# One decode step on one core: semaphores cleared beside the output's flight, and another order of loads in the last head

## The chip, the cores and the metric

One core of a Trainium2 chip. The metric is the device time of one execution in microseconds (us). The span that the profile shows runs from the first to the last instruction of the program; it is 1.7 to 2.9 us shorter than the time. The profile shows the granted clock of TensorE as a share of full speed: at every instant of the profile of before it is 1.0 or 0.5 (mean over the span 0.884).

## The reference

A token passes a layer norm, 32 heads of attention over 32,768 cached keys and values of 192 elements each, and an MLP of 640 to 1,536 to 640, with residuals.

```python
q = (layernorm(x) @ wq).reshape(B, Sq, H, Dh)         # 32 heads of 192
scores = einsum("bhqd,bhkd->bhqk", q, k_cache) * Dh ** -0.5
o = einsum("bhqk,bhkd->bhqd", softmax(scores), v_cache)
h = x + o.reshape(...) @ wo
out = h + relu(layernorm(h) @ w1) @ w2
```

The keys and values are 805 MB of the 825 MB that must be read.

## The kernel before

SyncE issues the loads (all but the token's own 1.25 KB) from one list. GpSimd passes on their arrivals. Per head, TensorE transposes a part of the keys and scores them, ScalarE copies the transposed keys out of PSUM and takes exponentials, VectorE scores the rest of the keys by multiplying and reducing, and TensorE sums the values. The last head is cut into ten chunks, numbered 0 to 9, so that little is left to do when the stream ends. Its order of loads:

```python
        end_keys(2, 2 * P * JL, JL, "dk1")
        g.wait("PV", LAST - 1, NC - 1)                 # values of the head before are used
        end_values(1, 0, JL * Dh, "dva", "v", LAST, 1) # "second values": chunks 2 and 3
        for i, jl in enumerate(ENDJ):                  # "last keys": chunks 6 to 9
            end_keys(NL - 1 + i, k0, jl, f"dke{1 + i}")
        ...                                            # more values, then w1 and w2
        g.wait("y_row")
        load(out.rearrange("b s (c p) -> (b s c) p", p=P), y_row[:], "dout", "out")
        g.wait("out")                                  # SyncE waits for the output here
        g.do(lambda: nc.sync.nop())
```

TensorE in the last head (the argument after `h` is the chunk):

```python
        transposes(g, h, 5)
        scores_pe(g, h, 4)
        values(g, h, 2)
        scores_pe(g, h, 5)
        transposes(g, h, 6)
        values(g, h, 3)
        ...
        values(g, h, 4)
        scores_pe(g, h, 8)
        scores_pe(g, h, 9)
        for c in (5, 6, 7):
            values(g, h, c)
        den_mm(g, h)                                   # the softmax's denominator
        values(g, h, 8)
        values(g, h, 9)
```

ScalarE there copies a chunk's transposed keys (`copies`), then takes the exponential of TensorE's scores (`exp_pe`) and of VectorE's (`exp_dve`) of a chunk or two earlier, in one fixed order. At the end of the program the context `nc.cleanup_on_exit()` lets GpSimd clear the 40 semaphores and then makes all engines meet once more (at a meeting each engine waits until all have come); before it there is the meeting that ends the block, after it the exit of the critical section and the program's last meeting.

The softmax here doesn't subtract the row's maximum and nothing guards it: scores larger than these inputs give would overflow.

Of the kernel before, what the change touches and what calls it, by code (L numbers as in the profile page):

```python
# [80 lines left out]
def kernel(  # L81
# [12 lines left out]
    nc = tc.nc  # L94
# [3 lines left out]
    _, H, Sk, Dh = A_k_cache.shape  # L98
# [9 lines left out]
    JL = 64  # L108
# [5 lines left out]
    NC = 2 * NL  # L114
    NB = NC
    LAST = H - 1
# [11 lines left out]
    NCM = len(ends)  # L128

    def chunks(h):  # L130
        return ends if h == LAST else full
# [14 lines left out]
    wo_view = A_wo.rearrange("(g p b) n -> g p b n", p=P, b=3)  # L146

    ctx.enter_context(tc.tile_critical(name="decode", no_gpsimd_drain=True))
    ctx.enter_context(nc.cleanup_on_exit())

    def sbuf(name, shape, dtype, align=32):
        return ctx.enter_context(nc.sbuf_tensor(name, shape, dtype, align_bytes=align))
# [77 lines left out]
    def dma_program(g):  # L230
        def load(dst, src, sem, *label):
            g.do(lambda: nc.sync.dma_start(out=dst, in_=src), sem, label, by=16)

        def rows(src, h, k0, jl):
            return src[h, k0:k0 + P * jl, :].rearrange("(p j) d -> p (j d)", p=P)

        def keys(h, ld):
            if h > 0:
                if ld == 0:
                    g.wait("PV", h - 1, 4 if h == 1 else 2)  # L240
                else:
                    g.wait("PV", h - 1, 5)
                g.wait("scs", h - 1, 4 * ld + 3)
            elif ld == 1:
                g.wait("att0")
            load(kt[ld][:], rows(k_hd, h, P * JK * ld, JK), f"dk{ld}", "k", h, ld)

        def vals(h, ld):

            if ld == 1:  # L250
                g.wait("PV", h, 1)
            elif h > 0:
                g.wait("PV", h - 1, 3 if ld == 0 else NC - 1)
            src = rows(v_hd, h, P * JK * (ld // 2), JK)
            if ld < 2:
                src = src[:, ld * JL * Dh:(ld + 1) * JL * Dh]
            load((vb, vb, va)[ld][:], src, "dva" if ld == 2 else "dvb", "v", h, ld)

        for c in range(DT):
            load(wq_c[c], wq_view[:, c * H * Dh:(c + 1) * H * Dh], f"dwq{c}", "wq", c)  # L260
        for h in range(LAST):
            keys(h, 0)
            vals(h, 0)
            keys(h, 1)
            for ld in ((2, 1) if h == 0 else (1, 2)):
                vals(h, ld)
            if h % 2 == 0:
                if h > 0:
                    g.wait("prj", h)
                load(wo_s[:], wo_view[h // 2], "dwo", "wo", h // 2)  # L270

        def end_keys(i, k0, jl, sem):
            load(k_at[i], rows(k_hd, LAST, k0, jl), sem, "k", LAST, i)

        def end_values(ld, c0, c1, sem, *label):
            load(v_at[ld][:, c0:c1], rows(v_hd, LAST, P * JL * ld, JL)[:, c0:c1], sem, *label)


        g.wait("PV", LAST - 1, 2)
        g.wait("scs", LAST - 1, 3)  # L280
        end_keys(0, 0, JL, "dk0")
        g.wait("PV", LAST - 1, 3)
        end_values(0, 0, JL * Dh, "dvb", "v", LAST, 0)
        end_keys(1, P * JL, JL, "dke0")
        g.wait("PV", LAST - 1, 5)
        g.wait("scs", LAST - 1, NC - 1)
        end_keys(2, 2 * P * JL, JL, "dk1")
        g.wait("PV", LAST - 1, NC - 1)
        end_values(1, 0, JL * Dh, "dva", "v", LAST, 1)
        k0 = P * JL * (NL - 1)  # L290
        at = []
        for i, jl in enumerate(ENDJ):
            at.append((k0, jl))
            end_keys(NL - 1 + i, k0, jl, f"dke{1 + i}")
            k0 += P * jl

        for i in range(2):
            end_values(2, i * J * Dh, (i + 1) * J * Dh, f"dvh{i}", "vh", i)
        i = 0
        for ld, (k0, jl) in enumerate(at):  # L300
            for c, (l, off, jc, *_) in enumerate(ends):
                if l == NL - 1 + ld:
                    g.wait("PV", LAST, 1)
                    load(v_tile(LAST, l)[:, off * Dh:(off + jc) * Dh],
                         rows(v_hd, LAST, k0, jl)[:, off * Dh:(off + jc) * Dh], f"dve{i}", "vc", LAST, c)
                    i += 1
        g.wait("PV", LAST, 3)
        load(w1_s, B_w1.rearrange("(c p) n -> p c n", p=P), "dw1", "w1")
        for i, (c0, c1) in enumerate(zip(W2_CUTS[:-1], W2_CUTS[1:])):
            load(w2_s[:, c0:c1], B_w2.rearrange("(c p) n -> p c n", p=P)[:, c0:c1], f"dw2_{i}", "w2", i)  # L310
        g.wait("y_row")
        load(out.rearrange("b s (c p) -> (b s c) p", p=P), y_row[:], "dout", "out")
        g.wait("out")
        g.do(lambda: nc.sync.nop())


    def pool_program(g):
# [225 lines left out]
    def pe_end(g):  # L543
        h = LAST
        den_mm(g, h - 1)
        transposes(g, h, 0)
        transposes(g, h, 1)
        scores_pe(g, h, 0)
        values(g, h, 0)
        scores_pe(g, h, 1)  # L550
        transposes(g, h, 2)
        o_turn(g, h - 1)
        values(g, h, 1)
        scores_pe(g, h, 2)
        transposes(g, h, 3)
        transposes(g, h, 4)
        scores_pe(g, h, 3)
        transposes(g, h, 5)
        scores_pe(g, h, 4)
        values(g, h, 2)  # L560
        scores_pe(g, h, 5)
        transposes(g, h, 6)
        values(g, h, 3)
        transposes(g, h, 7)
        scores_pe(g, h, 6)
        transposes(g, h, 8)
        scores_pe(g, h, 7)
        transposes(g, h, 9)
        values(g, h, 4)
        scores_pe(g, h, 8)  # L570
        scores_pe(g, h, 9)
        for c in (5, 6, 7):
            values(g, h, c)
        den_mm(g, h)
        values(g, h, 8)
        values(g, h, 9)
        o_turn(g, h)
        project(g, h + 1)
        st = ln_t["ln2"]["st"]
        g.wait("h_col")  # L580
        pe_group(g, [mmul(mm[:, 0:1], mean_mat[:], st[:, 0:1], start=True, stop=True)], ("mean", "ln2"), "pe_dve")
        g.wait("st", "ln2")
        pe_group(g, [mmul(sp[:, 0:2], mean_mat[:], st[:], start=True, stop=True)], ("mean2",), "pe_dve")
        g.wait("xn", "ln2")
        g.wait("w1")
        hn = ln_t["ln2"]["xn"]
        pe_group(g, [mmul(o_ps[:, f:f + 1], w1_s[:, c, f * P:(f + 1) * P], hn[:, c:c + 1],
                          start=(c == 0), stop=(c == DT - 1)) for f in range(FT) for c in range(DT)], ("h1",), "pe_act")
        g.wait("h1T")
        for i, (f0, f1) in enumerate(zip(W2_CUTS[:-1], W2_CUTS[1:])):  # L590
            g.wait("w2", i)
            pe_group(g, [mmul(attT[:, n:n + 1], w2_s[:, f, n * P:(n + 1) * P], h1T[:, f:f + 1],
                              start=(f == 0 and n == 0), stop=(f == FT - 1 and n == DT - 1), skip_group_check=True)
                         for f in range(f0, f1) for n in range(DT)], ("y", i), "pe_dve")
        g.wait("y_col")
        pe_group(g, [lambda: pe.transpose(out=mm[0:DT, 0:P], in_=y_col[:], identity=ident_f[:])], ("yT",), "pe_dve")
# [28 lines left out]
    def q_wide(g, h):  # L625
        g.wait("qs", h)
        if h > 0:
            g.wait("sc", h - 1, NC - 1)
        g.do(lambda: act.copy(out=qb[:], in_=mm[:, 0:Dh]), "act_dve", ("qb", h))
        g.do(lambda: act.copy(out=qm[:], in_=mm[:, Dh:Dh + 12]), "act_pe", ("qm", h))  # L630
# [12 lines left out]

    def act_head(g, h):
        q_wide(g, h)

        n = len(chunks(h))
        for c in range(n):
            if c == 4 and h < LAST:
                exp_pe(g, h, 3)  # L650
                exp_dve(g, h, 3)
                copies(g, h, 4)
                continue
            copies(g, h, c)
            if h == LAST:
                if c > 2:
                    exp_pe(g, h, c - 1)
                if c > 5:
                    exp_dve(g, h, c - 2)
                if c < 2:  # L660
                    exp_pe(g, h, c)
                    exp_dve(g, h, c)
                elif 2 < c < 5:
                    exp_dve(g, h, c - 1)
            elif c > 0:
                exp_pe(g, h, c - 1)
                exp_dve(g, h, c - 1)
        exp_pe(g, h, n - 1)
        if h == LAST:
            exp_dve(g, h, n - 2)  # L670
        exp_dve(g, h, n - 1)

    def act_end(g):
        act_head(g, LAST)
# [202 lines left out]
            looped("pe", nc.tensor)  # L877


# [1 line left out]
_INS = ['A_x', 'A_k_cache', 'A_v_cache', 'A_wq', 'A_wo', 'B_x', 'B_w1', 'B_w2']  # L881
_OUTS = [((1, 1, 640), 'bfloat16')]
# [25 lines left out]
```

## Time and profile before

| | before |
|---|---|
| time, median of 3 | 1918.56 us (1918.42 to 1918.67) |
| span of the profiled execution | 1916.9 us |
| loads' queue | 99.8% of the span |
| VectorE, TensorE, ScalarE busy | 82%, 81%, 49% |
| last head's first keys landed | 1849.97 us |
| denominator's matmul starts | 1903.35 us |
| output issued | 1913.29 us |
| last instruction ends | 1916.92 us |

A kernel with a full load queue is read from its end. The four last rows are the marks that profiles are compared by. The first comes from the semaphore records of the landings, the others from the order in time.

### The profile page before, as it was taken

To read this page: it belongs to the slowest core of one execution; us is meant where nothing else is said; L and a number is where in the kernel's file an instruction comes from. 1 tells how busy PE (TensorE), PEld (TensorE's weight loads), DVE (VectorE), ACT (ScalarE), POOL (GpSimd) and SP (SyncE) were. 2 spreads that over 40 slices of the span, in tenths; PEclk is the share of its full clock that TensorE was granted. 3 is DMA by queue.
4 is the path that set the end of the run, shared out by engine and by line. 5 is a ranking of instruction groups with operands and counts; after the bars stand their busy time and mean duration, and the time that the engine had idled before them with its cause. 6 is when DMAs were issued, how large, how long until landed. Compare 5 with 4: busy or idle time off the path is not lost.

```text
span 1916.9 us, 36096 instructions
## 1 busy us (share of the span) xinstructions
PE 1549.2 (81%) x15890; PEld 1083.9 (57%) x15890; DVE 1563.2 (82%) x732; ACT 938.9 (49%) x1998; POOL 1.0 (0%) x6
## 2 busy tenths in 40 slices
PE   7778787887878788878878877878778787878887
PEld 7555555655555555555556555556555555555555
DVE  2797787987878978789787888878798787887897
ACT  2455454554544544545545445445455454454454
POOL 0000000000000000000000000000000000000000
PEclk9888998888988889888899888899888898888988
DMA  9999999999999999999999999999999999999998
GB/s 408 429 432 434 429 437 428 439 432 432 434 435 431 434 436 428 436 431 438 433 434 435 432 433 434 435 428 438 429 437 434 432 436 432 433 435 433 430 430 354
DMA packets 29634, 825.29 MB, mean 431 GB/s; under 512 B 3115, under 2 KB 4652, under 8 KB 8108
## 3 DMA queue, kind: packets, MB, share of 16 engines
q1 hardware_dynamic: 29610, 824.98, 99.8%
q8 instruction: 15, 0.25, 0.0%
q14 instruction: 7, 0.06, 0.0%
q10 hardware_dynamic: 2, 0.00, 0.0%
HBM read 824.97 MB, written 0.00 MB: 430 GB/s over the span
## 4 chain that ended last, share of the span: by engine, by line
DVE 42%; DMA 37%; PE 14%; ACT 5%; issue 1%; DVEq 0%; POOLq 0%; SPq 0%
DMA kt<-in_A_k_cache_dram 35%; DVE sc L704 20%; DVE pr L701 20%; PE o_ps L364 7%; PE tp L383 6%; ACT kT L607 5%; DMA va<-in_A_v_cache_dram 2%; DVE o_pair L716 1%; PE sp L364 1%; ACT pA L622 0%; DVE oT L726 0%; DMA kt<-in_A_wq_dram 0%; DVE rec L709 0%; DVE rec L710 0%; DVE odd L722 0%
## 5 line engine op out<-in xcount | busy, mean ns | idle before, releaser
L701 DVE TENSOR_TENSOR pr<-kt,qb 128x3072 f32<-128x3072 bf16 (+2 forms) x257 | 757.5, 2947 | 314.8 <-POOLq L325 286.7
L607 ACT COPY kT<-tp 128x1024 bf16<-128x1024 bf16 (+1 forms) x897 | 813.2, 1016 | 277.3 <-PE tp L383 277.2
L383 PE MATMUL tp<-ident_f,kt 128*128 128x128 f32 x3453 | 586.2, 330 | 239.5 <-POOLq L346 164.2
L704 DVE TENSOR_REDUCE sc<-pr 128x16 f32<-128x3072 f32 (+2 forms) x257 | 756.9, 2945 | 8.9
L383 PEld LDWEIGHTS tp<-ident_f,kt 128*128 128x128 f32 x3453 | 481.2, 170 | 290.8 <-POOLq L346 169.7
L364 PE MATMUL o_ps<-va,pB 128*2 128x384 bf16 x1150 | 221.3, 340 | 66.2 <-POOLq L346 66.2
L364 PEld LDWEIGHTS sp<-qm,kT 128*128 128x128 bf16 x6906 | 197.4, 98 | 84.0 <-issue 43.0
L364 PE MATMUL sp<-qm,kT 128*128 128x2 bf16 x6906 | 214.4, 164 | 26.6 <-ACT pB L613 25.2
L364 PE MATMUL o_ps<-vb,pB 128*2 128x384 bf16 x1152 | 213.6, 331 | 23.1 <-ACT pA L622 22.5
L622 ACT ACTIVATE pA<-sc 128x16 bf16<-128x16 f32 (+2 forms) x257 | 58.1, 226 | 350.3 <-DVEq L65 350.2
L613 ACT ACTIVATE pB<-sp 128x16 bf16<-128x16 f32 (+2 forms) x258 | 51.9, 201 | 303.8 <-PE sp L364 303.8
L364 PEld LDWEIGHTS o_ps<-va,pB 128*2 128x2 bf16 x1150 | 93.9, 86 | 161.8 <-POOLq L346 73.7
L364 PE MATMUL o_ps<-va,pA 128*2 128x384 bf16 x898 | 173.5, 335 | 0.0
L364 PE MATMUL o_ps<-vb,pA 128*2 128x384 bf16 x896 | 166.7, 326 | 0.0
L364 PEld LDWEIGHTS o_ps<-vb,pB 128*2 128x2 bf16 x1152 | 90.0, 84 | 122.3 <-ACT pA L622 28.4
L364 PEld LDWEIGHTS o_ps<-va,pA 128*2 128x2 bf16 x898 | 77.7, 87 | 77.1 <-issue 11.3
L364 PEld LDWEIGHTS o_ps<-vb,pA 128*2 128x2 bf16 x896 | 75.3, 84 | 70.3
L613 ACT ACTIVATION_READ_ACCUMULATOR pB<-sp 128x1 f32 x258 | 54.7, 212 | 0.0
L622 ACT ACTIVATION_READ_ACCUMULATOR pA<-sc 128x1 f32 x257 | 52.9, 206 | 0.0
L364 PE MATMUL o_ps<-xn_ln,kt 128*96 128x1 bf16 (+1 forms) x316 | 22.3, 208 | 2.7 <-DMA kt<-in_A_wq_dram 2.7
L364 PEld LDWEIGHTS o_ps<-xn_ln,kt 128*96 128x96 bf16 (+1 forms) x316 | 22.1, 174 | 2.9 <-issue 2.7
L716 DVE TENSOR_SCALAR o_pair<-o_ps,rec 2x384 bf16<-2x384 f32 x32 | 19.3, 605 | 2.8 <-PE o_ps L364 1.7
(69 smaller groups left out, 186.6 us busy)
## 6 DMA issues: line engine op xcount, KB each, us to landing
kt<-in_A_k_cache_dram SPq DMA_DIRECT2D x62, 6144.0 KB, 26.7
vb<-in_A_v_cache_dram SPq DMA_DIRECT2D x63, 3072.0 KB, 20.8
va<-in_A_v_cache_dram SPq DMA_DIRECT2D x31, 6144.0 KB, 26.8
kt<-in_A_k_cache_dram SPq DMA_DIRECT2D x3, 3072.0 KB, 21.4
wo_s<-in_A_wo_dram SPq DMA_DIRECT2D x16, 480.0 KB, 19.0
kt<-in_A_wq_dram SPq DMA_DIRECT2D x4, 1536.0 KB, 10.9
va<-in_A_v_cache_dram SPq DMA_DIRECT2D x1, 3072.0 KB, 23.5
va<-in_A_v_cache_dram SPq DMA_DIRECT2D x2, 1536.0 KB, 34.6
```

What stands on the lines that cost most here:

```text
L364: return lambda: pe.matmul(o, lhsT=w, rhs=r, **kw)
L383: calls.append(lambda b=b, o=o: pe.transpose(out=dst[:, b, :], in_=src[:, o:o + 2 * P].bitcast(f32), identity=ident_f[:]))
L607: g.do(lambda: act.copy(out=kT[c % 2][:, b0:b0 + nb, :], in_=src[:, 0:nb, :].bitcast(bf16)), "act_pe", ("cp", h, c, k))
L613: g.do(lambda: act.activation(out=pB[c % NB][:, 0:jp], in_=sp[:, 0:jp], func=F.Exp, scale=SCALE, accum_out=dsums[:, 2 * c + 1:2 * c + 2]), ...
L622: g.do(lambda: act.activation(out=pA[c % NB][:, 0:jd], in_=sc[c % NC][:, 0:jd], func=F.Exp, scale=SCALE, accum_out=dsums[:, 2 * c:2 * c + ...
L701: g.chain(lambda: dve.tensor_tensor(out=pr[:, 0:j1 - j0, :], in0=src[:, (off + j0) * Dh:(off + j1) * Dh].rearrange("p (j d) -> p j d", d=D ...
L704: g.chain(lambda: dve.reduce_sum(out=sc[c % NC][:, j0:j1], in_=pr[:, 0:j1 - j0, :], axis=X), "dve")
L716: g.do(lambda: dve.tensor_scalar_mul(out=o_pair[:, :, 1, :], in0=o_ps[0:2, 0:2 * Dh].rearrange("q (i d) -> q i d", i=2), scalar1=rec[0:2, ...
```

## The change

Two parts. The close: GpSimd clears all semaphores but the output's while the output is on its way, SyncE waits for the output last and takes its semaphore back to zero by a decrement, and the second meeting falls away. The last head: the last keys load ahead of the second values, and TensorE and ScalarE get orders that suit this.

```diff
-    ctx.enter_context(nc.cleanup_on_exit())
+    before = nc.snapshot_sems()
...
-        g.wait("PV", LAST - 1, NC - 1)
-        end_values(1, 0, JL * Dh, "dva", "v", LAST, 1)
         k0 = P * JL * (NL - 1)
         ...                                  (the last keys)
+        g.wait("PV", LAST - 1, NC - 1)
+        end_values(1, 0, JL * Dh, "dva", "v", LAST, 1)
...
-        g.wait("out")
-        g.do(lambda: nc.sync.nop())
...
         scores_pe(g, h, 4)
-        values(g, h, 2)
+        transposes(g, h, 6)
         scores_pe(g, h, 5)
-        transposes(g, h, 6)
-        values(g, h, 3)
         transposes(g, h, 7)
         scores_pe(g, h, 6)
         transposes(g, h, 8)
         scores_pe(g, h, 7)
         transposes(g, h, 9)
+        values(g, h, 2)
+        scores_pe(g, h, 8)
+        values(g, h, 3)
+        scores_pe(g, h, 9)
         values(g, h, 4)
-        scores_pe(g, h, 8)
-        scores_pe(g, h, 9)
...
+        behind = ((0,), (1,), (), (2,), (), (), (3,), (), (4,), ())
+        for c in range(NCM):                 (ScalarE, last head)
             copies(g, h, c)
+            if c < 2:
+                exp_pe(g, h, c)
+            elif c > 2:
+                exp_pe(g, h, c - 1)
+            for d in behind[c]:
+                exp_dve(g, h, d)
+        exp_pe(g, h, NCM - 1)
+        for c in range(5, NCM):
+            exp_dve(g, h, c)
...
+    nc.clear_and_free_semaphores([n for n in nc.allocated_since(before) if n != sems["dout"].num])
+    nc.sync.wait_ge(sems["dout"], 16)
+    nc.sync.sem_inc(sems["dout"], -16)
```

So ScalarE no longer stands at an exponential that VectorE has yet to feed while copies are ready: exponentials of VectorE's chunks 3 and 4 come two places later, those of 5 to 7 after everything else.

## The prediction

> **What bounds the kernel now.** The page comes first. The row of DMA shares in the 40 slices and the main queue's line say that the loads fill the span:
>
> ```profile
> DMA  9999999999999999999999999999999999999998
> ...
> q1 hardware_dynamic: 29610, 824.98, 99.8%
> ```
>
> The bytes do not change (only the order of four loads does), so everything up to the last load, some 1910 us, is out of reach. What the change can move is what comes after the stream, and whatever in the last head keeps the engines from finishing as soon as the stream does. So I read the last 70 us: first the chain of waits (start, length, what), from the arrival of the last head's first keys.
>
> ```profile
> 1833.88 16.09 DMA kt<-in_A_k_cache_dram
> ...
> 1891.48 1.77 DVE pr L701
> 1893.27 1.76 DVE sc L704
> ...
> 1895.11 0.30 ACT pA L622 x2
> 1895.41 1.39 ACT kT L607 x2
> 1896.80 0.18 ACT pB L613 x2
> 1896.98 0.05 issue
> 1897.03 0.45 PE sp L364 x12
> 1897.48 5.94 PE o_ps L364 x36
> 1903.42 0.33 PE mm L364 x2
> ```
>
> The keys land at 1849.97 and VectorE then multiplies and reduces almost without a gap until 1895.03. There the chain leaves it: ScalarE turns VectorE's scores of chunk 6 into weights, and only then copies the transposed keys of chunk 9, TensorE scores chunk 9, and 36 value matmuls and the denominator's matmul queue up behind. VectorE itself ends later, but is not what the denominator waited for. The order in time of the same stretch (start, length, engine, line, operation, in brackets the idle time before it and who ended it) shows both:
>
> ```profile
> 1879.24 0.22 ACT L622 ACTIVATE pA<-sc 128x16 bf16<-128x16 f32 x1 [2.10 <-DVEq L65]
> 1879.45 2.82 ACT L607 COPY kT<-tp 128x1024 bf16<-128x1024 bf16 x3
> 1879.52 2.72 PE L364 MATMUL o_ps<-va,pB 128*2 128x384 bf16 x8 [1.42 <-POOLq L346]
> ...
> 1900.73 1.75 DVE L704 TENSOR_REDUCE sc<-pr 128x8 f32<-128x1536 f32 x1
> 1902.57 0.21 ACT L622 ACTIVATE pA<-sc 128x8 bf16<-128x8 f32 x1 [3.31 <-DVEq L65]
> 1903.35 0.40 PE L364 MATMUL mm<-dsums,ones_mat 128*128 128x20 f32 x2
> ```
>
> ScalarE sat 2.10 us before 1879.24 with copies ready behind an exponential that VectorE had not fed; TensorE waited 1.42 us for the second values (they land at 1879.42, by the semaphore records). At the end, ScalarE's last exponential is through at 1902.88 (its accumulator read), the denominator starts at 1903.35: 0.47 us that TensorE's own queue costs.
>
> Third, the issues (size, time to landing):
>
> ```profile
> kt<-in_B_w_dram SPq DMA_DIRECT2D x1, 320.0 KB, 17.4
> ```
>
> and SyncE's waits (in total, times, longest):
>
> ```profile
> SPq L858 <- DMA out_dram<-y_row: 0.8, 1, 0.8
> SPq _compat.py:109 <- PEq _compat.py:109: 0.6, 1, 0.6
> ```
>
> The last piece of w2 is issued at 1894.20 and lands 17.4 us later, at 1911.58; the ten matmuls that need it start at 1911.89. So the stream's own end is only 0.31 us ahead of the compute that uses it. The other two lines are the present close: SyncE waits for the output, and all engines then meet a second time for the clear.
>
> [...] The output here is issued at 1913.29 and SyncE goes on at 1914.51, 1.22 us; I use that.
>
> **The change, part 1: the close.** The sequencers' records of before read: output issued 1913.29 to 1913.65; landed 1914.51; first meeting of the engines released 1914.90; GpSimd's clear of the semaphores (0.25 us) and the second meeting until 1915.57; SyncE opens the exit of the critical section at 1915.63; end 1916.92. After: SyncE reaches the first meeting right after the issue. From the end of its wait to the release took 0.39 us (1914.51 to 1914.90), so the release falls near 1913.65 + 0.39 = 1914.04, and GpSimd clears two ranges (the output's semaphore lies between them), at most 2 x 0.25 us plus starts, by about 1914.7, beside the flight. SyncE gets its landing at 1914.51 as before; the branch that carries the wait and the decrement take about 0.2 us (0.16 from that branch to the next record of SyncE before), so it opens the exit near 1914.70 in place of 1915.63. The exit and the final meeting (1915.63 to 1916.92, 1.29 us) stay. Gain 0.93 us, entirely on the path.
>
> **Part 2: the last head.** The keys of chunks 6 to 9 (3 MB) and the second values (3 MB) swap places in a full queue. Intervals between landings in before: values 7.23 us, then keys 4.56, 1.83 and 0.92. After the third keys' 1872.19 the last keys therefore land at 1876.75, 1878.58 and 1879.50, the values at 1886.7. No gap should open: issue is earlier, and the queue then holds over 13 us of work. VectorE reaches chunk 6 at 1891.48, long after either arrival, so its end, 1902.48, stays. The first weights of the MLP are issued when value chunk 3 is done, now some 4 us later than 1888.39; they landed 18.2 us after issue, behind 13 us of other bytes, so that is hidden.
>
> ScalarE runs ahead: chunk 5's copies start at 1877.1 and not 1879.45. With rows of before (1024 wide 0.95 us, a pair of exponential and read 0.30): copies of 5 until 1879.95, of 6 1882.45, of 7 1885.25, of 8 1887.05, of 9 1889.15, exponentials between them. TensorE's last transposes (chunk 9) follow scores 7, near 1886.2, and are done at 1887.1. Then value chunks 2 to 7 stand in a row with scores 8 and 9: four of 16 matmuls and two of 10, 84 x 0.163 = 13.7 us, plus 2 x 0.45 for the scores. At full clock they end at 1901.7, and the denominator waits for VectorE and ScalarE alone: 1902.88 plus 0.06 (what a TensorE start after ScalarE costs at 1891.42) = 1902.94, 0.41 us earlier than 1903.35.
>
> Of those 0.41 not all arrive: the last w2 piece lands at 1911.58, plus 0.05 of waking, so its ten matmuls start at 1911.63 at the earliest and not 1911.89: at most 0.26 us.
>
> And the full clock is not certain. Between 1879.2 and 1886.2 TensorE would do only 15 transposes[...]. [...] 1.2 are slack. So the denominator starts between 1902.94 and 1904.3,[...] at about 1903.35: as before. That kernel had the same trouble, seen in the windows (length, TensorE busy, weight loads, VectorE, ScalarE, GpSimd, granted clock, DMA share, GB/s):
>
> ```profile
> 1880.00:1885.00 5.00, 5.00 (x44) 2.60 (x43) 4.82 (x3) 2.45 (x5) 0.00 (x0) 0.71 1.00 421
> ```
>
> Sum: part 1 gives 0.93 us; part 2 between 0.26 us gained and 0.95 us lost, with a middle near zero. 1918.56 - 0.93 = 1917.6 us.
>
> **Rivals.** (a) The reorder gains fully. If TensorE kept its clock, the denominator would follow VectorE and w2's landing would be the bound: 1918.56 - 0.93 - 0.26 = 1917.4. The 1.2 us of slack speak for it, the thin transposes against. (b) The late second values hurt: value chunk 2 starts 7.6 us later (1887.1 for 1879.52), all value work is squeezed into the last 16 us, [...]: 1918.5. For it speaks that before had 1.42 us of waiting early and afterwards only short idle times, which still were worth something as slack. (c) The close is not hidden: if GpSimd's two clears are slower than read, or the exit waits for it, half of the 0.93 goes: 1918.1. Against it, GpSimd is needed only at the exit's last step, 0.5 us after its opening. (d) The stream gets a gap since the MLP's weights are issued 4 us later; it would cost its own length. Against it stand the 13 us of queue.
>
> **Range and chances.** The three runs of before lie within 0.25 us. [...] the close 0.2, another run's stream a few tenths: 1916.9 to 1918.5. Two per cent would be 38 us, and nothing here is worth over 2, so within 2% is all but sure: 0.99.
>
> **What would show it.** Right: in the profile of after the last VectorE reduce still ends about 52.5 us after the last head's first keys land; the wait of ScalarE before chunk 5's copies is gone; the last keys land about 7 us earlier and the second values about 7 us later; the denominator starts within 0.1 us of ScalarE's last read, or behind a stretch of half clock; from the output's issue to the end it is about 2.7 us and not 3.63, with GpSimd's clears inside the flight. Wrong: a slice with a DMA share under 0.9 before the end, a VectorE wait inside the last head, or a close that is not shorter.

The sum is 0.93 us gained by the close and, for the last head, between 0.26 us gained and 0.95 us lost with a middle near zero: 1918.56 - 0.93 = 1917.6 us. The latest start of the denominator, 1904.3, the 0.95 us lost (1904.3 less the 1903.35 of before), the middle at 1903.35 and a part of the range's width stand as estimates without their working. Two smaller estimates come from the profile before: the 0.05 us of waking (TensorE started 0.06 us after ScalarE at 1891.42, SyncE 0.04 us after GpSimd's release of the first meeting), and the 13 us of queue (the last piece ahead of w1's first, issued at 1888.39, landed at 1901.96).

## The result, and the profile after

The changed kernel takes 1918.59 us (median of 6, 1918.28 to 1919.30), the kernel before 1919.03 us (6 executions, 1918.42 to 1920.32; three of them are those of the table above, the three new ones took 1919.38 or more). The ratio is 0.9997, with a 95% interval from 0.9984 to 1.001: the same. A ratio is the mean time of one kernel's fast runs over that of the other's of the same rounds, so it is not quite the ratio of the medians.

The page of the changed kernel shows the stream as full as before:

```profile
DMA  9999999999999999999999999999999999999998
...
q1 hardware_dynamic: 29610, 824.98, 99.8%
```

Nothing was lost to a gap in the loads. The span is 1915.52 us in place of 1916.92. The chain of waits at its end (start, length, what) now reads:

```profile
1900.77 1.76 DVE sc L701
...
1902.61 0.31 ACT pA L620 x2
...
1902.96 0.40 PE mm L362 x2
1903.36 2.05 PE o_ps L362 x12
```

In the kernel before, this stretch of the chain ran through ScalarE's copies and 36 value matmuls of TensorE. Now it runs from VectorE's last reduce through ScalarE's last exponential to the denominator, with nothing queued between. The order in time shows what made that so:

```profile
1877.00 2.91 ACT L605 COPY kT<-tp 128x1024 bf16<-128x1024 bf16 x3
...
1886.57 1.46 PE L362 MATMUL o_ps<-va,pB 128*2 128x384 bf16 x8 [0.38 <-POOLq L344]
...
1902.96 0.40 PE L362 MATMUL mm<-dsums,ones_mat 128*128 128x20 f32 x2 [1.64 <-ACT pA L620]
```

ScalarE copies chunk 5 at 1877.00 (1879.45 before). The second values come late (value chunk 2 starts at 1886.57, before at 1879.52), and still TensorE has waited 1.64 us when the denominator's operand arrives. That wait is harmless: it means that VectorE and ScalarE are the bound and TensorE is not.

The issues (size, time to landing) of the second values, the last keys' first piece and the last piece of w2 (23.5, 27.7 and 17.4 us to landing before):

```profile
va<-in_A_v_cache_dram SPq DMA_DIRECT2D x1, 3072.0 KB, 32.1
...
kt<-in_A_k_cache_dram SPq DMA_DIRECT2D x1, 1920.0 KB, 27.0
...
kt<-in_B_w_dram SPq DMA_DIRECT2D x1, 320.0 KB, 16.8
```

The swap shows in the landings by the semaphore records: the last keys' first piece at 1876.49 (1883.98 before), the second values at 1886.47 (1879.42 before). SyncE's waits at the end:

```profile
SPq L904 <- PEq L904: 0.5, 2, 0.4
SPq L879 <- SPq L879: 0.4, 1, 0.4
```

The 0.6 us of the second meeting are gone, and of the 0.8 us for the output 0.4 are left; the view puts that wait down to SyncE's own queue, since it waits there for its own transfer. The sequencers' records give the times: output issued 1913.19, first meeting released 1913.98, GpSimd's two clears from 1914.14 to 1914.57, SyncE past the landing at 1914.40, exit opened at 1914.47, end 1915.52.

| mark (us) | before | after |
|---|---|---|
| last head's first keys landed | 1849.97 | 1850.02 |
| from there to VectorE's last reduce | 52.51 | 52.50 |
| from there to the denominator | 53.38 | 52.95 |
| from the denominator to the output's issue | 9.94 | 10.22 |
| output's issue to the end | 3.63 | 2.33 |

Of the span's 1.40 us, 1.30 come from the close. The last head brought the denominator 0.43 us nearer, but the stretch behind it took 0.28 us more. Two things are seen there. TensorE's clock fell to half at 1908.0 (1910.2 before), so from the start of w1's matmuls to ScalarE's use of them it is 1.79 us and not 1.69. And there is one pause among the matmuls of w2:

```profile
1910.29 1.54 PE attT L362 x52
1911.83 0.03 issue
1911.86 0.37 PE attT L362 x8
```

Two of these start 0.19 us apart where 0.03 is usual; from the first of them to VectorE's use of the sum it is 1.96 us and not 1.79. No wait explains the pause and no other profile repeats it.

### The profile page after: what moved, and what is told of

It reads as the page before. It is cut to its first block, busy times and chain, and to the rows that moved or that the text cites. A ratio compares the mean times of both kernels' runs of the same rounds, so it can differ in the third digit from the quotient of the medians.

```text
span 1915.5 us, 36089 instructions
## 1 busy us (share of the span) xinstructions
PE 1554.6 (81%) x15890; PEld 1091.6 (57%) x15890; DVE 1563.2 (82%) x732; ACT 938.5 (49%) x1998; POOL 1.0 (0%) x6
## 3 DMA queue, kind: packets, MB, share of 16 engines
q1 hardware_dynamic: 29610, 824.98, 99.8%
## 4 chain that ended last, share of the span: by engine, by line
DVE 42%; DMA 37%; PE 14%; ACT 5%; issue 1%; DVEq 0%; POOLq 0%; SPq 0%
DMA kt<-in_A_k_cache_dram 35%; DVE sc L701 20%; DVE pr L698 20%; PE tp L381 7%; PE o_ps L362 6%; ACT kT L605 4%; DMA va<-in_A_v_cache_dram 2%; DVE o_pair L713 1%; PE sp L362 1%; ACT pA L620 0%; DVE oT L723 0%; DMA kt<-in_A_wq_dram 0%; DVE rec L706 0%; DVE rec L707 0%; DVE odd L719 0%
## 5 line engine op out<-in xcount | busy, mean ns | idle before, releaser
L381 PE MATMUL tp<-ident_f,kt 128*128 128x128 f32 x3453 | 592.3, 333 | 237.8 <-POOLq L344 162.9
L381 PEld LDWEIGHTS tp<-ident_f,kt 128*128 128x128 f32 x3453 | 489.0, 172 | 287.0 <-POOLq L344 168.9
```

Source lines behind the costliest of these rows:

```text
L381: calls.append(lambda b=b, o=o: pe.transpose(out=dst[:, b, :], in_=src[:, o:o + 2 * P].bitcast(f32), identity=ident_f[:]))
```

## The experiments

All twelve gave correct results. The granted clock and the arrival of the stream differ from execution to execution, so each kernel is judged by its marks more than by its time. This table holds one profile of each kernel; the last column tells whether and when TensorE's clock was at half between the transposes of chunk 5 and the denominator.

| kernel | median us (n) | first keys landed | keys to denominator | denominator to output | output to end | half from chunk 5 on |
|---|---|---|---|---|---|---|
| before | 1918.56 (3) | 1849.97 | 53.38 | 9.94 | 3.63 | 1879.5 to 1882.9 |
| after | 1918.59 (6) | 1850.02 | 52.95 | 10.22 | 2.33 | 1880.7 to 1884.1 |
| same_again | 1920.24 (5) | 1851.58 | 53.38 | 10.01 | 3.39 | no |
| after_again | 1918.82 (5) | 1849.98 | 53.87 | 10.25 | 2.33 | 1884.6 to 1891.4 |
| close_alone | 1919.33 (5) | 1851.29 | 55.06 | 9.95 | 2.33 | 1899.7 to 1903.1 |
| head_alone | 1919.42 (5) | 1850.41 | 53.83 | 9.93 | 3.38 | 1881.0 to 1891.3 |
| scalar_order_alone | 1921.02 (5) | 1849.75 | 55.92 | 10.28 | 3.39 | 1879.5 to 1883.0 |
| loads_alone | 1925.10 (4) | 1850.48 | 59.30 | 9.93 | 3.38 | 1879.7 to 1890.0 |
| engines_alone | 1922.19 (4) | 1850.44 | 56.25 | 9.99 | 3.38 | 1882.3 to 1889.1 |
| kept_warm | 1917.44 (6) | 1850.48 | 52.95 | 10.04 | 2.33 | no |
| no_second_meeting | 1918.98 (4) | 1850.10 | 53.38 | 9.97 | 2.89 | 1879.3 to 1882.7 |
| extra_meeting | 1919.86 (4) | 1850.77 | 52.96 | 10.05 | 2.73 | 1881.5 to 1884.9 |
| kept_warm_again | 1918.35 (5) | 1849.69 | 52.96 | 9.94 | 2.33 | no |
| kept_warm_to_the_end | 1918.08 (5) | 1851.11 | 52.95 | 9.90 | 2.32 | no |

The first job took same_again to head_alone, the second scalar_order_alone to kept_warm, the third the rest; each job ran its kernels on one chip, the first two on the same one. The kernel before has nine executions in the first job and nine in the third; the second job added only one, so its three kernels are compared with the first job's nine and that one. VectorE's last reduce ended 52.50 to 52.52 us after the first keys in every one of these profiles. The column of the first keys is the noise of the stream: 1.9 us between the extremes, more than the whole change is worth.

**same_again.** No edit.

> The kernel before, unchanged, timed against itself: a measure of the noise. The median of the two must agree within 0.5 us if differences of 1 us are to be read from times at all. Its span from the first to the last instruction is expected near 1916.9 us with a spread of about 1 us between executions. One profile of the changed kernel had a span of 1915.5 us at a time of 1918.3 us (2.8 us outside the span), one of the kernel before 1916.9 us at 1918.7 us (1.8 us outside). Theory A: the time outside the span is noise and varies from execution to execution in both kernels alike, 1.8 to 2.9 us. Rival B: it is 1.8 us for the kernel before always, and what the new close saves in the span is partly given back outside it; then every execution here has 1.8 us.

The kernel before against itself: 1920.24 us against 1919.24 (9 executions), ratio 1.0004 (0.9990 to 1.0017). The medians differ by 1.0 us, not by under 0.5: differences of a us can't be read from five executions. The time outside the span was 1.8 to 1.9 us in most, but 2.7 to 2.9 in two of these five and one of the nine. So theory A holds: that difference jumps in both kernels, and in the sixteen kept-warm executions below, which have the new close, it is 1.7 to 1.9 us, so nothing of the close comes back outside the span. The close took 3.39 us here, not 3.63.

**after_again.** No edit of the changed kernel.

> The changed kernel again. Theory A: time 1.0 to 1.4 us under the kernel before on the same chip (1.3 us from the close, 0.1 us from the last head), span near 1915.5 us, from the output's issue to the end 2.3 us again. Rival B: time only 0.0 to 0.5 us lower, since what the close saves inside the span comes back outside it (2.3 to 2.9 us outside in most executions). The denominator's matmul again starts within 0.1 us after ScalarE's last accumulator read, 52.9 to 53.0 us after the last head's first keys land, unless a stretch of half clock lies over the value matmuls, which would put it up to 1.4 us later.

1918.82 us against 1919.24, ratio 0.9994 (0.9980 to 1.0007). By the medians that is 0.42 us less, the rival's size, by the means 1.06, theory A's: these times alone do not decide between them. The close is 2.33 us again. The denominator came at 53.87 and not at 52.95, behind a long stretch of half clock. In the windows (length, TensorE busy, weight loads, VectorE, ScalarE, GpSimd, granted clock, DMA share, GB/s) value chunk 2, from 1887.00 on, runs at 0.50, and its first eight matmuls take 2.72 us in place of 1.46:

```profile
1880.00:1885.00 5.00, 3.74 (x64) 2.85 (x65) 4.82 (x3) 5.00 (x14) 0.00 (x0) 0.96 0.97 417
1885.00:1890.00 5.00, 4.83 (x33) 2.67 (x31) 4.97 (x2) 2.95 (x8) 0.00 (x0) 0.50 0.99 419
```

In the first profile of the changed kernel the second of these stretches was at full clock:

```profile
1885.00:1890.00 5.00, 4.62 (x55) 2.78 (x54) 4.96 (x2) 3.21 (x10) 0.00 (x0) 1.00 1.00 421
```

**close_alone.**

```diff
 the kernel before, with
-    ctx.enter_context(nc.cleanup_on_exit())
+    before = nc.snapshot_sems()
 and the three lines at the end; g.wait("out") and the nop taken out
```

> Only the close is changed: semaphores cleared beside the output's flight, no second meeting, SyncE waits last; the last head as before. If the saving is all in the close: from output issue to end 2.3 us in place of 3.6 us, and the whole time as low as the changed kernel's within 0.3 us. If the last head matters as much, it is half a us slower than the changed kernel.

The close takes 2.33 us, as in the changed kernel: it does not need the last head. The time, 1919.33, is no better than that of before (ratio 0.9998, 0.9984 to 1.0011) and 0.51 us above after_again's, as expected if the last head matters as much; a difference of this size is within the noise just seen. The profile says what held its own execution up. With the old order of the last head, TensorE waited for ScalarE before scores 9, the clock dropped at 1899.65, and value chunk 5 ran at half:

```profile
1898.34 0.45 PE L362 MATMUL sp<-qm,kT 128*128 128x2 bf16 x12 [2.00 <-ACT pB L611]
...
1900.38 2.77 PE L362 MATMUL o_ps<-va,pA 128*2 128x384 bf16 x8
1902.94 1.21 PE L362 MATMUL o_ps<-vb,pB 128*2 128x384 bf16 x6
```

Eight matmuls take 2.77 us; at full clock they take 1.46. The denominator came at 55.06. So the kernel before has its own bad case: of four profiles of its last head three read 53.38 and this one 55.06.

**head_alone.** The changed kernel with the old close.

> Only the last head is changed (order of loads, TensorE, ScalarE); the close is as before. My theory: the denominator starts at VectorE's end plus 0.48 us, 0.4 us earlier than before relative to the last head's first keys, but the output is issued only 0.0 to 0.3 us earlier, so the time is that of the kernel before within 0.3 us. Rival: the last head gives the 0.4 us in full, and time and output issue are 0.4 us lower.

The denominator came at 53.83, behind half clock from 1881.0 to 1891.3, so neither theory could be seen at work; the close is 3.38. What both had in common fell: the 0.4 us are not a property of the order alone but of order and clock. The time is 1919.42 (ratio 0.9998, 0.9984 to 1.0012).

**scalar_order_alone.** The kernel before with ScalarE's new `act_head`; nothing else.

> The kernel before with ScalarE's new order in the last head alone; loads, TensorE's order and the close as before. Theory: the half us in front of the denominator came from ScalarE's FIFO alone (copies of chunk 9 behind the exponential that VectorE feeds at 45 us), so this kernel starts the denominator within 0.1 us after ScalarE's last accumulator read, 52.9 to 53.0 us after the first keys of the last head, as the changed kernel does in a lucky phase of the clock, and it needs no other order of loads. Rival: the second values and the last keys still come in the old order, TensorE still waits for the values at chunk 2 and for the keys at chunk 6, and the denominator comes 53.4 us or later after the first keys, as in the kernel before.

My theory fell. The denominator came at 55.92 and the time is 1921.02 (ratio 1.0009, 0.9995 to 1.0022). In the order in time:

```profile
1884.85 2.20 ACT L607 COPY kT<-tp 128x1024 bf16<-128x1024 bf16 x3 [5.03 <-PE tp L383]
...
1887.48 1.46 PE L364 MATMUL o_ps<-va,pB 128*2 128x384 bf16 x8 [2.12 <-ACT pA L622]
```

ScalarE's new order puts the exponential of chunk 3 behind the copies of chunk 6. These wait 5.03 us for TensorE's transposes, which stand behind value chunk 2. Then TensorE's value chunk 3 waits 2.12 us for that exponential. These two queues serve each other and had to be reordered together: the new order of one alone made both wait, 5.03 and 2.12 us.

**loads_alone.** The kernel before with the two blocks of loads swapped.

> The kernel before with the order of the loads changed alone. TensorE's program then meets value chunk 2 before the transposes of chunk 6 and waits there for values that land 7 us later, near 36.5 us after the first keys. I expect the denominator some 57 us after the first keys (18 us of TensorE work and 2 to 3 us of waits after 36.5) in place of 53.4, and 3.5 to 5 us more time than the kernel before. Rival: TensorE has enough slack to hide the 7 us, and the time stays within 1 us.

TensorE stood 8.43 us at value chunk 2, the denominator came at 59.30 and the time is 1925.10 (ratio 1.0028, 1.0013 to 1.0043):

```profile
1887.03 2.72 PE L364 MATMUL o_ps<-va,pB 128*2 128x384 bf16 x8 [8.43 <-POOLq L346]
1889.54 1.68 PE L364 MATMUL o_ps<-va,pA 128*2 128x384 bf16 x8
```

I expected 57, and 3.5 to 5 us more time, where it is 5.5: the wait was as foreseen, but the work behind it took longer, with half clock until 1890.0.

**engines_alone.** The kernel before with TensorE's and ScalarE's new orders and the old loads.

> The kernel before with the new orders of TensorE and ScalarE, the loads in the old order. TensorE meets the transposes of chunk 6 before value chunk 2 and waits for keys that land 34 us after the first ones. In the changed kernel 8.2 us lie between the start of those transposes and value chunk 2, then 14.6 us to the denominator: some 57 us after the first keys, 3 to 4.5 us more time than the kernel before, with half clock over a part of it. Rival: within 1 us.

TensorE stood 4.45 us at the transposes of chunk 6; denominator at 56.25, time 1922.19 (ratio 1.0015, 1.0000 to 1.0031):

```profile
1884.53 2.19 PE L383 MATMUL tp<-ident_f,kt 128*128 128x128 f32 x9 [4.45 <-DMA kt<-in_A_k_cache_dram]
```

I expected some 57, and 3 to 4.5 us more time, where it is 2.6.

So the loads alone, ScalarE's order alone, and both engines' orders without the loads each lose by the mark (one profile each); by the time alone only loads_alone is clear of 1. The swap of the loads pays for the order of the engines. TensorE's order alone was not run, nor the change without TensorE's or without ScalarE's part, so whether each of these is needed is not shown.

**kept_warm.** The changed kernel with matmuls whose result nobody reads, in the gaps where TensorE waits for ScalarE.

```diff
+    def warm(g):
+        for _ in range(12):
+            g.do(mmul(o_ps[0:HE, 384:512], ident_b[:, 0:HE], wide[:, 0:128], start=False, stop=False, skip_group_check=True))
...
         transposes(g, h, 6)
+        warm(g)
         scores_pe(g, h, 5)
         transposes(g, h, 7)
+        warm(g)
         scores_pe(g, h, 6)
         transposes(g, h, 8)
+        warm(g)
         scores_pe(g, h, 7)
```

> The changed kernel with 3 x 12 matmuls of 128 columns put into TensorE's idle stretches between the last transposes and scores, written to unused columns; the result is the same. If the half clock over these stretches is what moved the denominator from 52.95 us after the first keys (one profile of the changed kernel) to 53.87 us (another), then here the granted clock is 1.0 from chunk 5's transposes until the denominator, and this starts 52.9 to 53.0 us after the first keys in the profile; the time is 0.0 to 0.7 us below the changed kernel's. Rival: the extra matmuls cost as much as they save (36 x 0.06 = 2.2 us of TensorE against 1.2 us of slack), and the denominator is later than 53.5 us.

(The 0.06 us of a matmul is an estimate: the value matmuls, three times as wide, start 0.163 us apart at full clock in the profile before, a third of which is 0.054.)

The clock stays at 1.00 and the denominator is at 52.95:

```profile
1880.00:1885.00 5.00, 4.78 (x90) 4.40 (x88) 4.91 (x2) 5.00 (x16) 0.00 (x0) 1.00 0.98 422
1885.00:1890.00 5.00, 4.53 (x56) 2.71 (x54) 4.88 (x2) 3.41 (x11) 0.00 (x0) 1.00 0.97 411
```

and in the order in time TensorE's longest wait before the denominator is for ScalarE, at the end (the other is 0.4 us for the second values):

```profile
1903.43 0.40 PE L362 MATMUL mm<-dsums,ones_mat 128*128 128x20 f32 x2 [1.64 <-ACT pA L627]
```

The time is 1917.44 against 1919.58 for the kernel before, ratio 0.9989 (0.9977 to 1.0002). The 36 matmuls cost nothing: TensorE still waits 1.64 us for ScalarE at the end.

**kept_warm_again.** The same kernel, in the third job.

> The changed kernel with the 36 extra matmuls, once more[...]. Theory: the granted clock is 1.0 throughout the last head's chunks 5 to 9 in this profile too and the denominator starts 52.9 to 53.0 us after the first keys; median time 1.5 to 2.5 us below the kernel before. Rival: the first profile was a lucky phase; [...] the denominator is 53.2 us or later.

Full clock again, denominator at 52.96; 1918.35 us against 1919.39, ratio 0.9995 (0.9981 to 1.0009). The time misses the expected 1.5 to 2.5 us below; the mark holds.

**kept_warm_to_the_end.** As kept_warm, and:

```diff
         values(g, h, 9)
+        for _ in range(6):
+            g.do(mmul(tp[0][:, 0:2, :], ident_b, wide[:, 0:256], start=True, stop=True))
         o_turn(g, h)
+        for _ in range(3):
+            g.do(mmul(tp[0][:, 0:2, :], ident_b, wide[:, 0:256], start=True, stop=True))
```

> As kept_warm, with 9 more matmuls of 256 columns in the two waits for VectorE after the last values, so that the MLP's first matmuls run at full clock more often. In the kept-warm profile the clock fell to half at 1908.9, and the 60 matmuls of w1 took 1.77 us from their start to ScalarE's use of them, where the kernel before, at full clock, took 1.69. Expected: 0.0 to 0.2 us from the denominator to the output's issue (10.04 us in the kept-warm profile), so 9.8 to 10.0; not to be seen in the times. If the extra matmuls stand in the way of the turn of the output, it is over 10.1.

9.90 us from the denominator to the output: within what was expected, and next to nothing against the 9.94 that kept_warm_again reached without it. Time 1918.08, ratio 0.9993 (0.9980 to 1.0007).

Taken together, the 16 executions of the three kept-warm kernels have a mean of 1917.92 us, the 19 of the kernel before that they were compared with (nine of these from the first job) 1919.60: 1.7 us less. The 11 of the changed kernel (its first rounds and after_again) have a mean of 1918.62, from other rounds. So the kept-warm version has the lowest times of those tried. Against the changed kernel the marks give 0.0 to 0.9 us (52.95 to 52.96 in three of three profiles, in place of 52.95 to 53.87 in four of the changed last head); the 0.7 us between the means are of other rounds and in part of another chip, and the two were never run side by side. The interval of each single ratio still includes 1.

The same pooling says more of the change itself than any single ratio: the 15 executions of the kernel before that the changed kernel's 11 were compared with have a mean of 1919.45 us (1919.68 with the five of same_again), 0.8 to 1.1 us more than 1918.62.

**no_second_meeting.** The kernel before, still waiting first, with a clear after the block and no meeting behind it.

```diff
-    ctx.enter_context(nc.cleanup_on_exit())
+    before = nc.snapshot_sems()
...
+    nc.clear_and_free_semaphores(nc.allocated_since(before))
```

> The kernel before without the second meeting of the engines: SyncE still waits for the output first, then all meet, then GpSimd clears all semaphores in one instruction and everyone goes to the exit. From the output's issue to the end the kernel before takes 3.39 us (three profiles, one more with 3.63), the changed one 2.33. The second meeting lasts 0.66 us from release to release, of which GpSimd's clear is 0.25; with the clear beside the exit I expect 2.75 to 2.95 us. If the order of the wait alone made the gain, it stays at 3.3 to 3.4.

2.89 us: 0.50 less than 3.39. The clear now lies beside the exit, which only at its last step waits for GpSimd (0.2 us).

**extra_meeting.** The changed kernel with `nc.all_engine_barrier()` after SyncE's decrement.

> The changed kernel with a meeting of all engines added after SyncE's wait. If the meeting is worth 0.4 us by itself (the first meeting took 0.39 us from the end of SyncE's wait to its release), from the output's issue to the end it takes 2.7 to 2.8 us in place of 2.33.

2.73 us: 0.40 more than 2.33. SyncE's waits show the meeting as a line of its own:

```profile
SPq L879 <- SPq L879: 0.4, 1, 0.4
SPq L880 <- PEq L880: 0.3, 1, 0.3
```

So the close's 1.06 us (3.39 to 2.33) split into 0.50 for the meeting dropped, and 0.56 for letting the first meeting and the clear run beside the flight. By the other path, waiting last with the clear beside the flight gives 0.66 (3.39 to 2.73) and dropping the meeting then 0.40. Why the two paths differ by 0.10 us was not taken apart. By the sequencers' records the added meeting was not free of waiting: SyncE came to it at 1915.08, GpSimd, which was at its second clear until 1915.16, at 1915.28.

## Why the prediction was right or wrong

**The bound: right.** The stream stayed full, and VectorE's chain in the last head kept its 52.5 us in fourteen of fourteen profiles.

**The close: right in mechanism, too small in two terms.** Counted from the output's issue, the release of the first meeting was put at 0.75 us and came at 0.80; GpSimd's clears were to be done by 1.41 and were by 1.38; the landing took 1.21 us (1.22 foreseen). Mis-sized was the reopening, "about 0.2 us": it took 0.07 (1914.40 to 1914.47); in the records the wait and the decrement are now one semaphore instruction, where a branch carried the wait before, 0.17 us ahead of SyncE's next record. And "the exit and the final meeting (1.29 us) stay" took its figure from an execution in which TensorE's drain in the exit was late; in all other profiles of that close the whole is 3.38 or 3.39, 0.24 less than the 3.63 I built on. The gain is 1.06 us in place of 0.93, and 1.30 against that one profile.

**The last head: the working held, one cap did not.** VectorE's end plus 0.46 was foreseen for a full clock (1902.94), and 0.44 came (1902.96); the arrivals came as worked out (last keys foreseen from 1876.75, landed from 1876.49; values foreseen at 1886.7, landed 1886.47). The half clock between the thin transposes was foreseen and appears in all four profiles of the changed last head, and the denominator's range, 52.97 to 54.33 us after the first keys, contains 53.87 and 53.83 and is missed by 0.01 to 0.02 by 52.95 and 52.96.

Its length was mis-sized: it was to last into the values (an estimate). So it did in after_again and head_alone (until 1891.4 and 1891.3), but in after and extra_meeting it ended at 1884.1 and 1884.9, ahead of the values. The 15 transposes did not spread evenly over the seven us: in these two profiles 13 and 14 of them ran within the 3.41 us of half clock. What makes the clock fall and come back is not shown. TensorE's busy time does not tell these two stretches apart: in the profile after it was busy for 2.64 of the 3.41 us before 1880.69, where the clock fell, and for 2.67 of the 3.41 us from 1884.10, after which the clock stayed full. kept_warm shows that it is the clock: with the gaps filled the clock stays full and the denominator is at 52.95 to 52.96 in three of three profiles. Since two of four reach that without the filling too, the count alone would be weak; it is the half clock over the values in the two late ones that carries the argument.

The step that failed is the cap, "the last w2 piece lands at 1911.58 [...] at most 0.26 us". It was taken from one landing that came 61.61 us after the first keys; over the fourteen profiles it came at 60.84 to 61.74. In the profile after it came at 60.84 and was there 0.78 us before the first of its ten matmuls (1911.64). The cap bound nothing. What took the gain instead, in that profile, is the slower stretch behind the denominator (0.28 us), of which 0.10 is the half clock over w1's matmuls and 0.17 the pause among w2's, which stays unexplained.

**The number.** 1917.6 was worked out from a median of 1918.56. In the result the kernel before had 1919.03, and the changed kernel 1918.59, which is 0.09 above the stated range; by the ratio it is 1918.56 x 0.9997 = 1918.0, inside. The expected 0.93 us of gain appear as 0.44 between the medians and 1.40 between the spans of one profile each, and as 0.8 to 1.1 in the pooled means. That part 2 came out near its foreseen middle of zero in the first profile (0.43 gained, 0.28 lost) is in part luck: the loss came from where none was foreseen. The noise of the stream, 1.9 us in the landing of the first keys, was the term that I set too low ("a few tenths").

**The rivals.** (a) and (b) are both seen at the denominator: the same kernel shows 52.95 and 53.87, with half clock until 1884.1 and until 1891.4; but w2's landing, which (a) made the next bound, was none. (c) did not come true: the second clear ran 0.17 us past the landing (1914.40 to 1914.57), but GpSimd was at the exit at 1914.61, before SyncE's step that waits for it (1914.76). (d) did not: w1 was issued at 1892.43 in place of 1888.39 and landed at 1905.92, earlier than before (1906.64).

## What to carry to other kernels

When the load queue is full for 99.8% of the span, look for gains only behind the last arrivals, and compare marks inside one profile (here: from the first keys of the last head), since the stream's own noise exceeds such gains. Reorder loads and the queues that serve each other together: the three partial versions tried took 1.4 to 5.5 us more by the medians here. Clear semaphores and meet while the last transfer is in flight (1.06 us of the close here; a clear of 40 semaphores took 0.25 us, of 20 and 19 0.14 and 0.13), and try filling short gaps of TensorE with idle work where the clock would otherwise be at half over a critical row of matmuls (up to 0.9 us at the denominator here, not shown in a side-by-side timing).
